# Gradient of the shift taps on VectorE over rows turned by DMA, and dh slab by slab ahead of dw, in a fused long-convolution and gated-MLP backward kernel

## The chip, the cores and the metric

One core of a Trainium2 chip runs the whole kernel. The metric is the device time of one execution in microseconds (us). Engines are written as in the profile: PE is TensorE, PEld its weight loads, DVE is VectorE, ACT is ScalarE, POOL is GpSimd, SP is SyncE, which only issues DMAs here.

## What is computed

The forward function takes x = q of shape 2048 x 1024 (rows s, channels d), normalises its rows, and forms two branches whose product is added to x. The reference returns that output and the gradients of nine of its inputs.

```python
def _A_ref(q, k, v, shift_k, ssm_k, ssm_D):
    for t in range(ks):                       # ks = 4: the shift taps
        k_shift = k_shift + k_pad[:, t:t + S, :] * shift_k[:, ks - 1 - t][None, None, :]
    kv = k_shift * v
    ...                                       # y: long causal convolution of kv with ssm_k, by FFT
    y = y + kv * ssm_D[None, None, :]
    return q * y
def _B_ref(x, w_gate, w_up, w_down):
    g = jnp.einsum("bsd,df->bsf", x, w_gate)
    u = jnp.einsum("bsd,df->bsf", x, w_up)
    return jnp.einsum("bsf,fd->bsd", g * u, w_down)
xn = _layernorm(x, axis=-1)
s = _A_ref(xn, A_k, A_v, A_shift_k, A_ssm_k, A_ssm_D)
g = _silu(_B_ref(xn, B_w_gate, B_w_up, B_w_down))
return x + s * g
...
_out, _vjp = jax.vjp(_f, A_q, A_k, A_v, A_shift_k, A_ssm_k, A_ssm_D, B_w_gate, B_w_up, B_w_down)
```

F is 3584. The gradient of the shift taps is, for each channel d and tap j, the sum over s of dkshift[s, d] * k[s - j, d].

## The kernel before, in words

A tile framework schedules the program: the author writes operations in an order, and a scheduler puts each engine's queue in an order of its own, by priorities and its own reckoning of times, unless an operation is marked to keep its place (`keep_in_program_order`, which PIN and PINQ switch on) or to follow another (`issue_after`). Each engine then works through its queue strictly in order, and so does each queue of DMA issues. Pools hand out buffers; a tile with one buffer is written again only when its last reader is done.

The work runs in five stages, in the time of the profiled execution:

1. *g and u* (0 to 580 us): PE multiplies the normalised rows by w_up and w_gate in 14 slabs of 256 columns (L585). The forward convolution is pumped in between (`conv_forward`, L608).
2. *bm* (580 to 775 us): h times w_down (L988), then `gate` (L993), which makes the output and the gradients dbm, dy, dxa.
3. *dh and dw* (775 to 1397 us): for each of 14 slabs, `dh_half` (L1108) computes two halves of dh = dbm times w_down transposed: per half, four PSUM tiles of 16 matmuls (L1119), copied by ACT (L1121), and two multiplications on DVE that turn the stored g and u into their gradients in place (L1126). `dw_slab` (L1132) then makes the weight gradients of the slab, eight groups of 16 matmuls (L1136), whose operands are both halves of the slab. The two are interleaved: after each dw group, half of a `dh_half` of the next slab is issued (`halves`, L1181), and its multiplication is issued behind the PSUM group after it (`todo`, `after_group`).
4. *dwd* (1397 to 1638 us): the gradient of w_down (L1244), 14 slabs of four groups. Each slab's h (1 MB) is loaded by SP (`load_h`, L1151), the results (wbs, four buffers) are stored by ACT's queue (L1249). Between the loads of h, SP issues DMA transposes of weights (`load_wgu`, L1199, 1 MB each) and of the stored gradients (`load_dgut`, L1204, two of 256 KB each) for the last stage. Transposes of weights wait for the latest issue of an h load.
5. *dx* (1638 to 2056 us): the gradient of the normalised rows (`dx_part`, L1264, matmuls L1267), 16 blocks of 128 rows in pairs; PSUM tile psx has three buffers. Each block ends with `ln_backward` (L1273): DVE adds psx and dxna into dxn (L1289), which frees psx, and the rest of the layer norm follows. While the second pair of every four blocks runs, SP reloads the 14 dgut pieces (28 transposes) for the next four.

The backward convolution (`conv_backward`, L838) is pumped into stages 3 and 4 by `btick`: 8 forward transforms of dy (`fwd8`, matmuls psF L230, whose PSUM is copied by ACT ahead, `fwd8_half` L268), then 16 units of product, inverse transform and matmuls (psY, L420 and L927). Its DVE work, the multiplications of stage 3 and the stores on POOL's queue are all marked to keep program order. The tail of an h unit (`dh_tail`, L918) copies PSUM by ACT in plain order into hr, and POOL turns it into ho (L931).

The gradients of k and of the shift taps come from `dk_units` (L936), pumped into stage 5: 16 units (8 groups of 128 channels, two halves of the rows). Each loads kh and dkh by POOL's queue, makes dk by seven operations on DVE (dka, dkp), and computes the taps on PE: 16 matmuls of dkh against four shifted views of kh (L964), accumulated in psdk over both halves. The taps are the diagonal of the result: DVE multiplies by `diag`, sums, and copies (L971 to L974).

Of the kernel before, what the change touches and what calls it, by code (L numbers as in the profile page):

```python
# [19 lines left out]
def build_kernel(  # L20
# [11 lines left out]
    nc = tc.nc  # L32
# [30 lines left out]
    PINQ = [False]  # L63

    def st(out, in_):
        ins = nc.gpsimd.dma_start(out=out, in_=in_)  # L66
        if PINQ[0]:
            tc.keep_in_program_order(ins)
        return ins
# [47 lines left out]
    ident_f = const.tile([P, P], F32, name="ident_f")  # L117
    make_identity(nc, ident_f[:])
# [9 lines left out]
    diag = const.tile([P, 64], F32, name="diag")  # L128
# [74 lines left out]
    PIN = [False]  # L203

    def tt(o, a, b, op):
        ins = V.tensor_tensor(o, a, b, op)  # L206
        if PIN[0]:
            tc.keep_in_program_order(ins)
# [53 lines left out]
    def stt(o, a, f, b):  # L262

        ins = V.scalar_tensor_tensor(o, a, f, b, op0=MUL, op1=ADD)
        if PIN[0]:
            tc.keep_in_program_order(ins)

    def fwd8_half(x, i, wp, psp):  # L268

        SP = wp.tile([P, 2, 2, 512], F32, name="SP", bufs=2)  # L270
        for j in range(2):
            r = 2 * i + j
            ps = psp.tile([P, 2, 2, 256], F32, name="psF")
            cmm(ps[:, 0], T4[0], x, (r,))
            cmm(ps[:, 1], T4[0], x, (r + 4,))
            nc.scalar.copy(out=SP[:, :, j], in_=ps[:].rearrange("p s k x -> p s (k x)"))
        return SP

    def fwd8(SPs, X, wp, ahead):

        W = wp.tile([P, 16, 256], F32, name="W16")
        C = wp.tile([P, 4, 256], F32, name="W4")
        for i in range(2):
            s, q = [SPs[i][:, j].rearrange("p a (k x) -> p (a k) x", k=2) for j in range(2)]
            tt(W[:, 4 * i:4 * i + 4, :], s, q, ADD)
            tt(W[:, 4 * i + 8:4 * i + 12, :], s, q, SUB)
            yield 2.5
        tt(C[:], W[:, 0:4, :], W[:, 4:8, :], ADD)
        tt(W[:, 0:4, :], W[:, 0:4, :], W[:, 4:8, :], SUB)
        ahead(0)  # L290
        yield 2.4
        dft4(C[:], W[:, 0:4, :], X, 0)
        ahead(1)
        yield 2.8

        d0, d2r = W[:, 8:10, :], W[:, 13:11:-1, :]
        tt(C[:, 0:2, :], d0, d2r, ADD)
        tt(d0, d0, d2r, SUB)
        re, im = W[:, 10:15:4, :], W[:, 11:16:4, :]
        tt(C[:, 2:4, :], re, im, ADD)  # L300
        tt(W[:, 12:14, :], im, re, SUB)
        yield 2.8
        q, pr_ = C[:, 2:4, :], W[:, 13:11:-1, :]
        tt(W[:, 10:12, :], q, pr_, ADD)
        tt(W[:, 14:16, :], q, pr_, SUB)
        stt(pr(X, 2, 15), W[:, 10:15:4, :], C8, C[:, 0:2, :])
        stt(pr(X, 10, 7), W[:, 10:15:4, :], -C8, C[:, 0:2, :])
        yield 2.9
        stt(pr(X, 6, 11), W[:, 11:16:4, :], C8, d0)
        stt(pr(X, 14, 3), W[:, 11:16:4, :], -C8, d0)  # L310
        yield 1.5
    FWD8_W = 2 * 2.5 + 2.4 + 2.8 + 2.8 + 2.9 + 1.5
# [428 lines left out]
    tt(diag[:], ident_f[:, 0:64], ident_f[:, 64:128], ADD)  # L741
# [74 lines left out]
    def dy_forward(cx, cs):  # L816
        def load(ds):
            if ds < 8:
                x = cx.tile([P, NB, P], BF16, name="dyx")
                cld(x[:], DYd[ds])  # L820
                xs_.append(x)
        xs_, sp = [], []

        def half(ds, i):
            if ds < 8:
                sp.append(fwd8_half(xs_[ds], i, cs, ps_c3))
        load(0)
        load(1)
        half(0, 0)
        half(0, 1)  # L830
        for ds in range(8):
            SPs = sp[2 * ds:2 * ds + 2]
            load(ds + 2)
            X = cs.tile([P, 16, 256], BF16, name="DX")
            yield from fwd8(SPs, X, cs, lambda i: half(ds + 1, i))
            st(DYFd[ds], X[:])

    def conv_backward():  # L838
# [54 lines left out]
        for n in range(16):  # L893
            yield from staggered(main(n), tl, 7.0)
            tl = tail(n)
# [6 lines left out]
    def dkv_tail(ds, G, tiles, ew):  # L902
        v, ksh = tiles
        y = ew.tile([P, NB, P], BF16, name="yl")
        for rp in range(4):
            ps = inv8_rows(G, ps_y4[0], rp)
            nc.scalar.copy(out=by_res(y[:], rp), in_=rowps(ps))
        yield 0.0
        yield 0.0
        tt(v[:], v[:], y[:], MUL)  # L910
        tt(ksh[:], ksh[:], y[:], MUL)
        for c in range(2):
            cs_ = slice(8 * c, 8 * c + 8)
            st(DKSHd[ds, 1024 * c:1024 * c + 1024, :].rearrange("(u r) d -> u r d", r=8), v[:, cs_, :])
            st(o_dv[:, c, :, ds * P:(ds + 1) * P], ksh[:, cs_, :])
        yield 2.5

    def dh_tail(ds, G, ew):  # L918
        hr = ew.tile([P, 2, 8, P], BF16, name="yl")
        ho = ew.tile([P, 2, P, 8], BF16, name="ho")  # L920
        for c in range(2):
            for rq in range(2):
# [6 lines left out]
                nc.scalar.activation(hr[:, c, 4 * rq:4 * rq + 4], ps[:], ACT.Copy, scale=WSC)  # L929
        yield 0.0  # L930
        nc.gpsimd.tensor_copy(ho[:], hr[:].rearrange("p c r u -> p c u r"))  # L931
        nc.gpsimd.tensor_copy(ddo[:, ds:ds + 1], hr[:, 0, 0, 0:1])
        st(o_dssmk[ds * P:(ds + 1) * P, :], ho[:].rearrange("p c u r -> p (c u r)"))
        yield 0.0

    def dk_units(ew, psp):  # L936
        def load(i):
            ds, c = divmod(i, 2)
            kh = ew.tile([P, 11, P], BF16, name="kh")
            cld_k(kh[:], c, ds)  # L940
            dk = ew.tile([P, 11, P], BF16, name="dkh")
            src = DKSHd[ds]
            cld(dk[:], bass.AP(src.tensor, src.offset + 1024 * c * P, [[8 * P, P], [P, 11], [1, P]]))
            return kh, dk

        kh, dk = load(0)
        yield 2
        for i in range(16):
# [11 lines left out]
            if c == 0:  # L960
                ps = psp.tile([P, 4, 64], F32, name="psdk")
            for r in range(8):
                for j in (slice(0, 64), slice(64, 128)):
                    nc.tensor.matmul(ps[j], dk[:, r, j], kh[:, r:r + 4, j],  # L964
                                     start=(c == 0 and r == 0), stop=(c == 1 and r == 7))
            yield 1
            if i < 15:
                kh, dk = load(i + 1)
            if c == 1:
                dt_ = ew.tile([P, 4, 64], F32, name="dt2")  # L970
                tt(dt_[:], ps[:], diag[:].unsqueeze(1).to_broadcast([P, 4, 64]), MUL)  # L971
                dr_ = ew.tile([P, 4], F32, name="dr2")
                V.tensor_reduce(dr_[:], dt_[:], AX.X, ADD)
                V.tensor_copy(dsko[:, ds, ::-1], dr_[:])  # L974
            yield 2
        st(o_dshk.rearrange("(c p) j -> p c j", p=P), dsko[:])
    DK_TOTAL = 2 + 16 * 6

    C_TOTAL = 8 * FWD8_W + 16 * (PROD_W + INV8_W) + 8 * 1.4 + 8 * 2.5
# [120 lines left out]
    todo = []  # L1100

    def after_group(n):
        flush(2)
        while todo:
            todo.pop(0)()
        btick(n)

    def dh_half(k, wdt):  # L1108
# [3 lines left out]
        for g in range(2):  # L1112
            dht = bg.tile([P, 4, SLW], BF16, name="dht", bufs=3)
            for e in range(2):
# [7 lines left out]
                after_group(1)  # L1122

            def multiply(g=g, dht=dht):
                bs = slice(4 * g, 4 * g + 4)
                tt(dgu[:, :, bs], dgu[:, :, bs], dht[:].unsqueeze(1).to_broadcast([P, 2, 4, SLW]), MUL)  # L1126
                if g == 1:
                    ld(DGd[sl, :, 1024 * hf:1024 * hf + 1024, :].rearrange("a (u b) f -> u a b f", u=P), dgu)
            todo.append(multiply)
            yield  # L1130

    def dw_slab(sl, dgus, others):  # L1132
        for dc in range(DC):
# [12 lines left out]
            after_group(2)  # L1146
            next(others, None)

    h_ld = [None]

    def load_h(sl):  # L1151
        h = u8(HSL[sl % 3], "p (b f) -> p b f", b=NB)
        h_ld[0] = ld(h, Hd[sl])
        hs[sl] = h
# [8 lines left out]
    for k in (3, 4):  # L1163
        gu_in(k)
    DBM = [u8(q, a=4) for q in (10, 8, 4, 5)]
    HSL = (3, 11, 6)
    hs = {}
    PIN[0] = PINQ[0] = True
    for k in range(2):
        run(dh_half(k, wdt))  # L1170
    todo.pop()()
    for sl in range(NSL):
        if sl + 2 < NSL:
            wdts.append(load_wdt(sl + 2))
        if sl + 1 == NSL:
# [4 lines left out]

        def halves():  # L1181
            for k in (2 * sl + 2, 2 * sl + 3):
                if k < 2 * NSL:
                    yield from dh_half(k, wdts[sl + 1])
        dw_slab(sl, [DGU[2 * sl], DGU[2 * sl + 1]], halves())
# [28 lines left out]
    for k in range(NSL):  # L1214
        if k + 2 < NSL:
            load_h(k + 2)
        with tc.issue_after(h_ld[0].ins):
# [4 lines left out]
        if k == 11:  # L1222

            bdrain()
            PIN[0] = PINQ[0] = False
# [13 lines left out]
        for f in range(2):  # L1239
# [9 lines left out]
            sta(o_dwd[f0:f0 + P, :], wbs)  # L1249
# [10 lines left out]
    ps_k = pool("ps_k", 1, space=PSUM)  # L1260
    kpump, kdrain = make_pump(dk_units(kw_, ps_k), DK_TOTAL)
# [68 lines left out]
    for p_ in (ps_k, ps_x, kw_, gs, gl, gd2, ub, ua, gd, gw):  # L1330
# [64 lines left out]
```

## Time and profile before

| What | Value |
|---|---|
| median of three runs | 2061.24 us (2058.28 to 2066.14) |
| profiled execution | 2058.28 us; its span 2056.5 us |
| busy, share of the span | PE 1969.5 us (96%), DVE 1434.8 (70%), ACT 647.8 (32%), POOL 343.7 (17%) |
| mean granted TensorE clock | 0.982 |
| chain that ended last, by line | psx L1267 18%, psb L1136 18%, psb L1119 8%, psb L1244 5%, SPq L1202 4%, psdk L964 1% |
| DMA | 440.74 MB, mean 214 GB/s |
| idle of PE ahead of L1244, released by the load of h | 20.2 us |
| idle of DVE ahead of dka, released by the load of dkh | 199.5 us, 15 times |

How to read it: busy times are sums over the span, so the stage has to be looked at before an engine is called the bound. A wait is the idle time of an engine just before an instruction, with what released it. The chain is followed back from the last instruction. "SPq" is time in which SP's queue was issuing a DMA.

### The profile page before, as it was taken

The numbers are of one execution on the slowest core, as the hardware profiler recorded it, in microseconds if no ns is written. First come the engines' busy times: TensorE is split into PE (matmuls) and PEld (weight loads), VectorE is DVE, ScalarE is ACT, GpSimd is POOL, SyncE is SP. The second block draws the span as 40 slices with busy tenths as digits, with TensorE's granted clock in tenths as the row PEclk, the third lists the DMA queues.
The fourth block names the chain that finished last, engine by engine and source line by source line (L and its number), as shares of the span: only waits on it lengthen the run. The fifth ranks groups of instructions, "written<-read, shape, count | busy, mean of one in ns | idle before, by whom it ended". The sixth has DMA issues, their size and how long they took to land.

```text
span 2056.5 us, 27740 instructions
## 1 busy us (share of the span) xinstructions
PE 1969.5 (96%) x11288; PEld 1054.7 (51%) x11288; DVE 1434.8 (70%) x1576; ACT 647.8 (32%) x954; POOL 343.7 (17%) x496
## 2 busy tenths in 40 slices
PE   6999999999999999999999999999879799999998
PEld 3455555545544446666566655654434344444443
DVE  6779898978836556886999899999953034434343
ACT  4655554546432234432222222221112101111112
POOL 3322222111112211001021212121102001010100
PEclk9999999999999999999999999999989899999999
DMA  9686666557699987655686997667997979393951
GB/s 294 217 285 218 214 212 215 197 183 244 231 289 293 290 284 259 222 196 212 237 268 225 253 253 228 241 212 206 142 242 149 205 182 209 118 195 93 189 114 57
DMA packets 422528, 440.74 MB, mean 214 GB/s; under 512 B 248960, under 2 KB 336824, under 8 KB 408576
## 3 DMA queue, kind: packets, MB, share of 16 engines
q1 hardware_dynamic: 329472, 211.06, 40.6%
q0 software_dynamic: 42112, 176.51, 26.7%
q10 hardware_dynamic: 50816, 51.39, 7.9%
q8 instruction: 88, 1.44, 0.3%
q14 instruction: 40, 0.33, 0.1%
HBM read 198.72 MB, written 189.83 MB: 189 GB/s over the span
## 4 chain that ended last, share of the span: by engine, by line
PE 60%; issue 17%; DVE 9%; SPq 5%; POOL 4%; DMA 4%; ACT 1%; ACTq 0%; POOLq 0%; DVEq 0%
PE psx L1267 18%; PE psb L1136 18%; PE psb L1119 8%; PE psg L585 5%; PE psb L1244 5%; SPq L1202 4%; DVE W L206 2%; DVE HX L206 2%; PE psF L230 2%; SPq L1209 1%; DVE m L206 1%; DVE KX L206 1%; PE psdk L964 1%; PE psY L420 1%; POOL HTd L66 1%
## 5 line engine op out<-in xcount | busy, mean ns | idle before, releaser
L585 PE MATMUL psg<-wslab,U 128*128 128x512 bf16 x1792 | 417.1, 385 | 8.4 <-ACT U L558 5.5
L1136 PE MATMUL psb<-U,U 128*128 128x512 bf16 x1792 | 396.9, 379 | 0.0
L1267 PE MATMUL psx<-U,dgut 128*128 128x512 bf16 x1536 | 337.2, 380 | 5.1 <-DVE dxn L206 3.4
L1267 PEld LDWEIGHTS <-dgut 128*128 128x128 bf16 x1792 | 174.5, 98 | 217.0 <-issue 10.7
L585 PEld LDWEIGHTS <-U 128*128 128x128 bf16 x1792 | 175.0, 99 | 201.8 <-issue 15.0
L1136 PEld LDWEIGHTS <-U 128*128 128x128 bf16 x1792 | 175.3, 98 | 199.0 <-issue 0.4
L1244 PE MATMUL psb<-U,U 128*128 128x512 bf16 x896 | 201.3, 387 | 28.8 <-DMA U<-Hd 20.2
L1119 PE MATMUL psb<-wdt,U 128*128 128x256 bf16 x1792 | 206.4, 273 | 1.1 <-ACT bm L1006 1.1
L587 ACT CAST gut<-psg 128x512 bf16<-128x512 f32 x224 | 131.4, 587 | 204.2 <-PE psg L585 189.8
L1119 PEld LDWEIGHTS <-U 128*128 128x128 bf16 x1792 | 175.6, 98 | 31.5 <-issue 1.4
L988 PE MATMUL psbm<-U,ht 128*128 128x512 bf16 x784 | 169.9, 379 | 0.0
L1141 ACT CAST wb<-psb 128x512 bf16<-128x512 f32 x112 | 65.6, 586 | 311.6 <-PE psb L1136 308.7
L1244 PEld LDWEIGHTS <-U 128*128 128x128 bf16 x896 | 88.9, 100 | 138.8 <-DMA U<-Hd 20.7
L206 DVE TENSOR_TENSOR W<-W 128x1024 f32<-128x1024 f32 (+1 forms) x144 | 149.8, 1059 | 3.0
L206 DVE TENSOR_TENSOR dka<-dkh,Wbc 128x1024 bf16<-128x1024 bf16 x16 | 11.1, 692 | 199.5 <-DMA dkh<-DKSHd 199.5
L206 DVE TENSOR_TENSOR W<-SP 128x1024 f32<-128x1024 f32 x96 | 112.4, 1221 | 43.5 <-ACT SP L245 33.6
L1290 ACT ACTIVATE dx_t<-dxn 128x1024 bf16<-128x1024 f32 (+1 forms) x17 | 17.1, 1007 | 342.8 <-DVE dxn L206 284.6
L988 PEld LDWEIGHTS <-ht 128*128 128x128 bf16 x784 | 76.6, 98 | 91.8
L1121 ACT CAST dht<-psb 128x512 bf16<-128x512 f32 x112 | 65.6, 586 | 118.2 <-PE psb L1119 106.5
L206 DVE TENSOR_TENSOR U<-U,dht 128x2048 bf16<-128x2048 bf16 x56 | 71.1, 1272 | 44.3 <-ACT dht L1121 44.3
L206 DVE TENSOR_TENSOR m<-A,B 128x2048 bf16<-128x2048 bf16 (+1 forms) x48 | 73.4, 1577 | 40.1 <-issue 23.5
L1246 ACT CAST wbs<-psb 128x512 bf16<-128x512 f32 x56 | 32.3, 587 | 197.4 <-PE psb L1244 147.2
(203 smaller groups left out, 2284.7 us busy)
## 6 DMA issues: line engine op xcount, KB each, us to landing
U<-GUd SPq DMA_DIRECT2D x28, 1024.0 KB, 8.2
DGd<-U SPq DMA_DIRECT2D x28, 1024.0 KB, 4.5
GUd<-gut ACTq DMA_DIRECT2D x54, 512.0 KB, 4.3
A<-DYFd POOLq DMA_DIRECT2D x16, 1024.0 KB, 8.9
out_dram<-wb ACTq DMA_DIRECT2D x112, 128.0 KB, 5.0
U<-Hd SPq DMA_DIRECT2D x14, 1024.0 KB, 6.7
Hd<-hN POOLq DMA_DIRECT2D x54, 256.0 KB, 4.1
HTd<-hT POOLq DMA_DIRECT2D x54, 256.0 KB, 4.0
```

Source lines behind the costliest of these rows:

```text
L206: ins = V.tensor_tensor(o, a, b, op)
L230: nc.tensor.matmul(ps[:, k].rearrange("p (c d) -> p c d", c=2), T[:, r, k, :], xr[:, r], start=(n == 0), stop=(n == len(rs) - 1 and (first ...
L585: gu_mm[0] = nc.tensor.matmul(ps[:], XNT[q][:, dc, qi * P:(qi + 1) * P], w[:, dc].rearrange("p a f -> p (a f)"), start=(dc == 0), stop=(dc ...
L587: nc.scalar.copy(out=gut[:, :, i], in_=ps[:].rearrange("p (a f) -> p a f", a=2))
L988: nc.tensor.matmul(ps[:, dh * 512:(dh + 1) * 512], ht(fc)[:, i * P:(i + 1) * P], WD[fc // 4][:, fc % 4, dh * 512:(dh + 1) * 512], start=(f ...
L1119: nc.tensor.matmul(ps[:, x * SLW:(x + 1) * SLW], DBMT[2 * hf + g][:, dc, (b % 4) * P:(b % 4 + 1) * P], wdt[:, dc, :], start=(dc == 0), sto ...
L1121: nc.scalar.copy(out=dht[:, 2 * e:2 * e + 2].rearrange("p b f -> p (b f)"), in_=ps[:])
L1136: nc.tensor.matmul(ps[:], XN[b // 4][:, b % 4, dc * P:(dc + 1) * P], dgus[b // 8][:, :, b % 8], start=(b == 0), stop=(b == NB - 1))
L1141: nc.scalar.copy(out=wb[:, dc % 2].rearrange("p a f -> p (a f)"), in_=ps[:])
L1202: nc.sync.dma_start_transpose(out=store, in_=(B_w_gate, B_w_up)[a][:, j * 512:(j + 1) * 512])
L1244: nc.tensor.matmul(ps[:], h[:, b, f * P:(f + 1) * P], DBM[b // 4][:, b % 4, dh * 512:(dh + 1) * 512], start=(b == 0), stop=(b == NB - 1))
L1267: nc.tensor.matmul(ps[:, dh * 512:(dh + 1) * 512], t[n][:, f, i * P:(i + 1) * P], WGU[n][:, f, dh * 512:(dh + 1) * 512], start=(n == 0 and ...
```

## The change

It has four parts.

*Taps.* `dk_units` no longer loads kh and no longer uses PE. For each unit SP loads k and the gradient dkshift once more by DMA transpose, as kT and dkT with channels on partitions and 1024 rows along the free axis (one buffer each). DVE computes each tap by one `scalar_tensor_tensor` with an accumulated sum over up to 1024 elements: four a unit, 64 in all, plus an addition of both halves. `diag`, `ident_f` and the pool ps_k go. The weights of the pump's steps change with it.

*dh.* `dh_half` is no longer a generator: a whole half is issued, its two multiplications at a raised priority, and `dw_slab` runs in one piece. The order is: second half of this slab, first half of the next, then dw of this slab.

*Order.* PIN and PINQ are gone: the scheduler orders DVE's and POOL's work. `fwd8` makes its own matmuls and PSUM copies instead of having them ahead. The lag of `staggered` goes from 7.0 to 6.0. `dh_tail` has ACT write ho with steps of eight elements, instead of POOL turning it.

*dwd.* Loads of h move from SP to ACT's queue, stores of wbs from ACT to SP's queue, and a transpose of weights waits for the issue of the latest store of wbs.

```diff
-        ins = nc.gpsimd.dma_start(out=out, in_=in_)
-        if PINQ[0]:
-            tc.keep_in_program_order(ins)
-        return ins
+        return nc.gpsimd.dma_start(out=out, in_=in_)
...
-    def fwd8(SPs, X, wp, ahead):
+    def fwd8(x, X, wp, psp):
...
         for i in range(2):
-            s, q = [SPs[i][:, j].rearrange("p a (k x) -> p (a k) x", k=2) for j in range(2)]
+            SP = wp.tile([P, 2, 2, 512], F32, name="SP", bufs=2)
+            for j in range(2):
+                r = 2 * i + j
+                ps = psp.tile([P, 2, 2, 256], F32, name="psF")
+                cmm(ps[:, 0], T4[0], x, (r,))
+                cmm(ps[:, 1], T4[0], x, (r + 4,))
+                nc.scalar.copy(out=SP[:, :, j], in_=ps[:].rearrange("p s k x -> p s (k x)"))
+                yield 0.1
+            s, q = [SP[:, j].rearrange("p a (k x) -> p (a k) x", k=2) for j in range(2)]
...
-                nc.scalar.activation(hr[:, c, 4 * rq:4 * rq + 4], ps[:], ACT.Copy, scale=WSC)
-        yield 0.0
-        nc.gpsimd.tensor_copy(ho[:], hr[:].rearrange("p c r u -> p c u r"))
-        nc.gpsimd.tensor_copy(ddo[:, ds:ds + 1], hr[:, 0, 0, 0:1])
+                nc.scalar.activation(ho[:, c, :, 4 * rq:4 * rq + 4].rearrange("p u r -> p r u"), ps[:], ACT.Copy, scale=WSC)
+        yield 0.4
+        nc.scalar.copy(out=ddo[:, ds:ds + 1], in_=ho[:, 0, 0, 0:1])
...
-            kh = ew.tile([P, 11, P], BF16, name="kh")
-            cld_k(kh[:], c, ds)
             dk = ew.tile([P, 11, P], BF16, name="dkh")
...
-            return kh, dk
+            kT = ew.tile([P, 1, 16 + H], BF16, name="kT")
+            t0 = 0 if c else 16
+            nc.sync.dma_start_transpose(out=kT[:, :, t0:], in_=kin[c * H - 16 + t0:c * H + H, ds * P:(ds + 1) * P])
+            dkT = ew.tile([P, 1, H], BF16, name="dkT")
+            nc.sync.dma_start_transpose(out=dkT[:], in_=DKSHd[ds, c * H:c * H + H, :])
+            return dk, kT, dkT
...
             if c == 0:
-                ps = psp.tile([P, 4, 64], F32, name="psdk")
-            for r in range(8):
-                for j in (slice(0, 64), slice(64, 128)):
-                    nc.tensor.matmul(ps[j], dk[:, r, j], kh[:, r:r + 4, j],
-                                     start=(c == 0 and r == 0), stop=(c == 1 and r == 7))
+                taps = ew.tile([P, 2, 4], F32, name="taps", bufs=2)
+            for m in range(4):
+                lo = 0 if c else 3 - m
+                prod = ew.tile([P, 8, P], BF16, name="dkp")
+                V.scalar_tensor_tensor(prod[:].rearrange("p r d -> p (r d)")[:, lo:H], dkT[:, 0, lo:H], 1.0,
+                                       kT[:, 0, 13 + m + lo:13 + m + H], op0=MUL, op1=MUL,
+                                       accum_out=taps[:, c, 3 - m:4 - m])
+                yield 1
+            if i < 15:
+                dk, kT, dkT = load(i + 1)
+            if c == 1:
+                tt(dsko[:, ds, :], taps[:, 0, :], taps[:, 1, :], ADD)
...
-                after_group(1)
-
-            def multiply(g=g, dht=dht):
-                bs = slice(4 * g, 4 * g + 4)
+                flush(2)
+                btick(1)
+            with tc.high_priority(60):
                 tt(dgu[:, :, bs], dgu[:, :, bs], dht[:].unsqueeze(1).to_broadcast([P, 2, 4, SLW]), MUL)
...
         h = u8(HSL[sl % 3], "p (b f) -> p b f", b=NB)
-        h_ld[0] = ld(h, Hd[sl])
+        sta(h, Hd[sl])
...
     for sl in range(NSL):
+        dgus = [first, dh_half(2 * sl + 1, wdts[sl])]
         if sl + 2 < NSL:
             wdts.append(load_wdt(sl + 2))
-        if sl + 1 == NSL:
+        if sl + 1 < NSL:
+            first = dh_half(2 * sl + 2, wdts[sl + 1])
+        else:
...
-        dw_slab(sl, [DGU[2 * sl], DGU[2 * sl + 1]], halves())
+        dw_slab(sl, dgus)
...
-        with tc.issue_after(h_ld[0].ins):
+        with tc.issue_after(wst.ins) if k > 0 else nullcontext():
...
-            sta(o_dwd[f0:f0 + P, :], wbs)
+            wst = ld(o_dwd[f0:f0 + P, :], wbs)
...
-    ps_k = pool("ps_k", 1, space=PSUM)
-    kpump, kdrain = make_pump(dk_units(kw_, ps_k), DK_TOTAL)
+    kpump, kdrain = make_pump(dk_units(kw_), DK_TOTAL)
```

## The prediction

> **What bounds the kernel now.** I read the table of stretches first, then the groups, then the timelines of SP and PE. The columns of the table: stretch, its length, busy us of PE, PEld, DVE, ACT and POOL, granted TensorE clock, DMA share, GB/s.
>
> ```profile
> 782.00:1397.00 615.00, 609.29 (x3848) 373.54 (x3846) 541.39 (x530) 179.80 (x294) 90.38 (x123) 0.99 0.72 230
> 1397.00:1638.00 241.00, 210.53 (x1070) 98.73 (x1069) 138.88 (x124) 42.85 (x77) 33.10 (x25) 0.93 0.95 186
> 1638.00:2056.50 418.50, 405.58 (x2038) 186.57 (x2037) 159.53 (x214) 57.50 (x85) 38.41 (x61) 0.99 0.69 146
> ```
>
> PE fills the first stretch (the dh and dw slabs) and the last (dx). The middle one (dwd) loses some 30 us, and there the DMA share is highest. So work that leaves PE in dx comes off the end, and a new PE wait anywhere adds to it. The groups of dx that the change touches or that price it:
>
> ```profile
> L964 PE MATMUL psdk<-kh,dkh 128*64 128x256 bf16 x256 | 17.2, 276 | 0.0
> ...
> L206 DVE TENSOR_TENSOR dkp<-dkh,Wbc 128x1024 bf16<-128x1024 bf16 x48 | 33.1, 689 | 0.9
> ...
> L1300 DVE SCALAR_TENSOR_TENSOR dx_t<-dxn,RSTN,dout_t 128x1024 bf16<-128x1024 f32 x15 | 19.3, 1284 | 0.4
> ```
>
> SP's timeline (start, us, then the operation) shows who stands behind whom on SP; the first three lines lie in dwd, the rest in dx:
>
> ```profile
> 1454.53 41.15 SPq L1202 DMA_TRANSPOSE U<-in_B_w_gate_dram  x1
> 1495.77 0.53 SPq L61 DMA_DIRECT2D U<-Hd  x1
> ...
> 1586.52 38.00 SPq L1209 DMA_TRANSPOSE dgut<-DGd  x12
> ...
> 1664.34 4.58 SPq L1202 DMA_TRANSPOSE U<-in_B_w_up_dram  x1
> 1669.15 0.39 SPq L61 DMA_DIRECT2D dxna_t<-DXNAd  x1
> ...
> 1706.84 34.46 SPq L1209 DMA_TRANSPOSE dgut<-DGd  x20
> ```
>
> A load of h stood 41 us behind a weight transpose: that is PE's largest hole (20.2 us before L1244, by the waits). Twenty dgut transposes of 256 KB held SP for 34.46 us, 1.72 each; alone one takes 1.22 to 1.30 to issue, and lands 4.7 us after issue in the median (3.4 to 23.6). Last, from PE's timeline, the one wait of PE in dx:
>
> ```profile
> 1845.99 12.02 PE L1267 MATMUL psx<-U,dgut 128*128 128x512 bf16 x48 [3.43 <-DVE dxn L206]
> ```
>
> Here dxn, the operation of VectorE that frees psx, stood behind a product that waited for the dkh load (8.37 us of DMA dkh in the chain just before). This is the mechanism that I expect to grow.
>
> **Part 1: psdk leaves PE.** In PE's timeline a group of 16 psdk matmuls starts at 1678.29 and the next psx at 1679.29: 1.00 us. 16 groups make **-16.0**, all on the path. The sums over the diagonal go as well, 8 x (0.42 + 0.42 + 0.17) = 8 us of DVE, worth nothing: DVE is busy 159.5 of 418.5 us there.
>
> **Part 2: 64 products with sums on DVE.** Nearest rows: 0.69 (a bf16 product of this size) and 1.28 (L1300, the same instruction with an f32 operand). I take 1.22, close to the same instruction: 4.9 us a unit, 78 in all. As throughput this hides in DVE's 259 idle us; it counts only inside the chain of part 4.
>
> **Part 3: 32 more transposes on SP.** kT and dkT hold 256 KB each like one dgut load, so I price them like it. 32 x 1.72 = 55 us of DMA in a stretch with a share of 0.69: room on the whole, none inside the dgut bursts (share 1.06 to 1.16 per 20 us).
>
> **Part 4: the wait added.** kT and dkT have one buffer. kT of unit i+1 waits on SP for the last sum of unit i, and what is queued behind it on SP (dgut, dxna, xn, dout) waits too; the sums of unit i+1 wait on DVE for both transposes, and dxn behind them, and PE for dxn. A unit's loop is two issues 2.6 + landing 4.7 + sums 4.9 = **12.2 us**; lower bound 2.4 + 3.4 + 2.8 = 8.6; with a landing of 23.6 it is 31. Before, PE itself held dk back, since psdk stood between psx groups (a unit every 1700.11 - 1678.29 = 21.8 us). That brake is gone, and in the order that the scheduler gives DVE, dk runs ahead. The first dxn stands behind units 0 to 4 and 6 of the 7 operations of unit 5's dka (before: behind units 0 and 1 and 5 operations of unit 2); the third dxn behind unit 8 and a sum of unit 9; the fifth behind unit 13.
> - First: unit 2's kT follows the last weight transposes and the first dxna, xn and dout. Those were out 32 us into dx (1670.3 against 1637.9), now with one transpose fewer ahead: 27. Three loops are 36.6, five operations of 0.69 and dxn 1.2 follow: 68.3. A pair of blocks is 224 matmuls of 0.2165 = 48.5 us of PE, and the third psx buffer gives 1.7: a hole of **18**.
> - Third: count from the first dxn's start. PE wants the third by 49.7. dout waits for dx_t, 7.3 us behind dxn before (1687.24 to 1694.52), with four sums between them now 13, and kT of unit 6 stands behind it. Three loops, then issue and landing of unit 9, 7.3; four dgut transposes stand between the halves of units 8 and 9, 6; a sum and dxn 2.4: 65.3, a hole of 15.6 in calm queues. The dgut burst runs just then, so I take **20**.
> - Fifth: no burst. 9 us of dgut and xn ahead of unit 10, four loops 48.8, dxn 1.2: 59 against 49.7, a hole of **9**.
> Together **+47**. With loops of 8.6 they are 7 + 3 + 0 = 10; with one landing of 23.6 in each of the first two, 85. After unit 15 nothing is left to wait for. The wait of 3.4 at 1845 is of this kind and is counted out: **-3.4**.
>
> **Part 5: weight transposes later.** kT of unit 1 waits on SP for the sums of unit 0, and five weight transposes stand behind it. Issued every 4.9 us (24.5 for five) and landing after 8.5 (median of the line) they come 8 to 28 us into dx; PE wants pieces 9 to 13 at 9 x 3.46 = 31 to 45. Some 17 us of cover: 0 to +20, I take **+5**.
>
> **Part 6: dh no longer interleaved.** I summed DVE's rows in its order between one slab's multiplies and the next, scaled by 0.945 (first multiply to end of convolution the sums make 735, the trace 676 busy and 20 of gaps). Before: 40 to 43 us a slab. After, from the fifth group on: 45, 49, 48, 44, 46, 44, 44, together 319, where PE needs 7 x 43.35 = 303 (1049.09 to 1092.44 in the chain). Following both sums, with DVE waiting for dh where it is early, DVE comes 7 us after PE's need at the eighth slab and 9.5 at the last; before it had 15 in hand. **+10**. Bounds: 0, and +35 (DVE stood idle 1 to 10% from 1000 to 1400, some 23 us in all; no slack takes that up now).
>
> **Part 7: dwd.** h loads move to ACT's queue, wbs stores to SP behind the weight transposes. The hole at 1482 to 1504, 22 us, loses its cause. A wbs store behind 41 us leaves PE 4 wbs of 6.9 and 4 psb of 3.45 = 41 of cover, less 18 (the stores' median landing in that stretch): some comes back. At the end, stores 22 to 24 stand behind 2 weight and 15 dgut transposes; a like row of them took 51 us (1573.64 to 1624.5), and PE loses some 15 there already. **-10**; bounds -24 and +25. The activation that writes ho in steps costs between 0.60 (L929) and 0.97 (a quarter of POOL's 3.89), x32; ACT is busy 18 to 30%, which hides it, and if not, 12 us. POOL loses 31 us that nobody on the path waited for.
>
> **Sum** against the profiled execution (2058.28; span 2056.5): -16.0 + 47 - 3.4 + 5 + 10 - 10 = +32.6, 2090.9. The median of the runs shown is 3.0 above that execution: **2094**.
>
> **A rule against the change.** The dgut row turns 8 blocks of 128x128 in 1.72 us. The Trainium skill, "VectorE: DVE Perf Modes", The three transpose paths, puts one block at 1309 ns by DMA and 390 by TensorE. By it a transpose would be 10.5 us, a loop 26, and the end near 2,240. For dgut's shape this trace disagrees; for rows of 256 bytes it shows nothing.
>
> **Rivals.**
> - *Faster.* The chain is short: unit 2's transposes out by 20 us (not 27) and loops of 8.6 leave the first dxn at 50.5, as PE wants it, and nothing after it late. Then 16, 3.4 and dwd's 22 come off: 2061.3 - 41.4 = **2020**. For: DMA is at 0.2 to 0.5 between bursts. Against: six weight transposes took SP 30 us after dx began. 0.13.
> - *No change*: loops of 8.6, all else as forecast: -16 - 3.4 + 10 + 5 + 10 - 10 = -4.4, **2057**. 0.14.
> - *Much slower*: two landings of 23.6 and part 6 at its bound: -16 - 3.4 + 85 + 5 + 35 - 10 = +95.6, **2157**. For: DVE is busy 97 and 96% from 1300 to 1500. 0.18.
> - The forecast, 2072 to 2130: 0.55.
> Chances with a bound of 0.5%, about what a measurement of this kernel can tell from no change: faster 0.13, within 0.14, slower 0.73. The range 2048 to 2150 leaves out most of the first and half of the third.
>
> **What would show it.** Waits of PE L1267 on DVE dxn in the first three pairs, falling; landings of kT and dkT near 5 us; no hole at L1244 that names U<-Hd; DVE nearly without idle from 1000 to 1400, and PE short of 100% by some 10 us there. Sums of 0.69, or units out on SP without gaps, break part 4; PE idle of over 35 us from 1000 to 1400 breaks part 6.

## The result, and the profile after

The changed kernel takes 2122.56 us (median of four runs, 2108.10 to 2126.82), 1.0284 of the kernel before (95% interval 1.0231 to 1.0337; its four runs beside it had a median of 2060.75). The forecast was 2094, slower, with a range to 2150. All ratios in this document are taken over the executions within 1.5% of the fastest of the same kernel. The profiled execution took 2123.78, its span 2121.8.

The table of stretches of the changed kernel, with the same three stages in its own times (columns as before: stretch, length, busy us of PE, PEld, DVE, ACT and POOL, granted TensorE clock, DMA share, GB/s):

```profile
782.00:1423.00 641.00, 617.64 (x3854) 375.84 (x3852) 544.39 (x543) 200.76 (x298) 75.74 (x118) 0.98 0.68 223
1423.00:1658.00 235.00, 207.36 (x1058) 97.64 (x1057) 113.49 (x112) 77.55 (x82) 8.20 (x14) 0.94 0.95 177
1658.00:2121.80 463.80, 395.53 (x1792) 177.09 (x1791) 227.72 (x325) 57.74 (x86) 29.80 (x45) 0.93 0.66 142
```

In dx PE runs fewer matmuls (x1792 for x2038), as meant, yet the stretch has grown from 418.5 to 463.8 and the clock has fallen from 0.99 to 0.93. dh and dw have grown too, dwd is shorter. From first matmul to first matmul of the next stage: dh and dw 625.6 to 650.7 (+25.1), dwd 240.5 to 235.1 (-5.4), dx 418.6 to 463.5 (+44.9); with 0.7 lost ahead of them this is the whole 65.3 between the spans.

The waits of PE in these stages (operation and line, what it waited for, us in total, times, longest):

```profile
PE psx L1222 <- DVE dxn L196: 51.7, 3, 27.9
PE psb L1099 <- DVE U L196: 16.1, 7, 4.1
PE psx L1222 <- ACT wbs L1202: 11.1, 1, 11.1
PE psb L1200 <- ACT wbs L1202: 10.1, 1, 10.1
PE psx L1222 <- DMA U<-in_B_w_up_dram: 6.8, 1, 6.8
PE psb L1200 <- DMA U<-Hd: 6.6, 1, 6.6
```

The single wait of 3.43 for dxn has become three that hold 51.7. PE's timeline has them falling from pair to pair, 27.90, 20.25, 3.51 us, and none after:

```profile
1698.17 21.51 PE L1222 MATMUL psx<-U,dgut 128*128 128x512 bf16 x88 [6.82 <-DMA U<-in_B_w_up_dram]
1747.58 17.25 PE L1222 MATMUL psx<-U,dgut 128*128 128x512 bf16 x72 [27.90 <-DVE dxn L196]
...
1817.89 17.93 PE L1222 MATMUL psx<-U,dgut 128*128 128x512 bf16 x72 [20.25 <-DVE dxn L196]
...
1872.13 15.70 PE L1222 MATMUL psx<-U,dgut 128*128 128x512 bf16 x72 [3.51 <-DVE dxn L196]
```

psdk is gone from the groups. What stands in its place, and one row that nobody had asked for:

```profile
L939 DVE SCALAR_TENSOR_TENSOR dkp<-dkT,kT 128x1024 bf16<-128x1024 bf16 (+2 forms) x64 | 78.3, 1223 | 64.4 <-DMA dkT<-DKSHd 63.1
L899 ACT ACTIVATE yl<-psY 128x512 bf16<-128x512 f32 x32 | 74.7, 2712 | 0.0
```

A sum takes 1.22 us, as taken, and DVE sat idle 63 us ahead of the sums for dkT. The second row is the write of ho in steps of eight elements: 2.71 us against 0.60 for the contiguous write before.

SP's timeline of the changed kernel at the start of dx (dx begins at 1658.3):

```profile
1666.61 1.30 SPq L915 DMA_TRANSPOSE kT<-in_A_k_dram  x1
1667.95 2.44 SPq L917 DMA_TRANSPOSE dkT<-DKSHd  x1
1670.49 4.32 SPq L1159 DMA_TRANSPOSE U<-in_B_w_gate_dram  x1
1674.91 0.53 SPq L61 DMA_DIRECT2D out_dram<-wbs  x1
1678.19 1.18 SPq L915 DMA_TRANSPOSE kT<-in_A_k_dram  x1
...
1711.83 1.19 SPq L915 DMA_TRANSPOSE kT<-in_A_k_dram  x1
1713.05 2.23 SPq L917 DMA_TRANSPOSE dkT<-DKSHd  x1
1722.46 1.16 SPq L915 DMA_TRANSPOSE kT<-in_A_k_dram  x1
...
1732.34 1.16 SPq L915 DMA_TRANSPOSE kT<-in_A_k_dram  x1
```

The second unit's kT waits from 1675 to 1678 for the first unit's sums, with five weight transposes and two stores of wbs behind it. Then, from 1711.83, units come every 10.6 and 9.9 us while dxn waits behind them on DVE. The first dxn starts at 1746.31, 88 us into dx, behind the sums of five units and six of the seven operations that make the sixth's dka, as the prediction had read the order; in the kernel before it started 49 us into dx.

### The profile page after: what moved, and what is told of

Same layout as the page of the kernel before. It is cut to its first block, busy times and chain, and to the rows that moved or that the text cites. A ratio compares the mean times of both kernels' runs of the same rounds, so it can differ in the third digit from the quotient of the medians.

```text
span 2121.8 us, 27360 instructions
## 1 busy us (share of the span) xinstructions
PE 1962.8 (93%) x11032; PEld 1045.7 (49%) x11032; DVE 1480.0 (70%) x1687; ACT 703.0 (33%) x962; POOL 294.3 (14%) x462
## 5 line engine op out<-in xcount | busy, mean ns | idle before, releaser
L1099 PE MATMUL psb<-U,U 128*128 128x512 bf16 x1792 | 399.1, 383 | 16.1 <-DVE U L196 16.1
L1222 PE MATMUL psx<-U,dgut 128*128 128x512 bf16 x1536 | 341.9, 385 | 69.6 <-DVE dxn L196 51.7
L1099 PEld LDWEIGHTS <-U 128*128 128x128 bf16 x1792 | 176.7, 99 | 226.4 <-issue 25.8
L1084 PE MATMUL psb<-wdt,U 128*128 128x256 bf16 x1792 | 199.8, 273 | 1.1 <-ACT bm L978 1.1
L196 DVE TENSOR_TENSOR W<-W 128x1024 f32<-128x1024 f32 (+1 forms) x144 | 139.2, 986 | 2.8
L939 DVE SCALAR_TENSOR_TENSOR dkp<-dkT,kT 128x1024 bf16<-128x1024 bf16 (+2 forms) x64 | 78.3, 1223 | 64.4 <-DMA dkT<-DKSHd 63.1
L196 DVE TENSOR_TENSOR dxn<-psx,dxna_t 128x1024 f32<-128x1024 f32 (+1 forms) x17 | 19.7, 1160 | 126.5 <-PE psx L1222 122.7
L1086 ACT CAST dht<-psb 128x512 bf16<-128x512 f32 x112 | 65.3, 586 | 128.9 <-PE psb L1084 105.7
```

What stands on the lines that cost most here:

```text
L939: V.scalar_tensor_tensor(prod[:].rearrange("p r d -> p (r d)")[:, lo:H], dkT[:, 0, lo:H], 1.0, kT[:, 0, 13 + m + lo:13 + m + H], op0=MUL, ...
L1084: nc.tensor.matmul(ps[:, x * SLW:(x + 1) * SLW], DBMT[2 * hf + g][:, dc, (b % 4) * P:(b % 4 + 1) * P], wdt[:, dc, :], start=(dc == 0), sto ...
L1086: nc.scalar.copy(out=dht[:, 2 * e:2 * e + 2].rearrange("p b f -> p (b f)"), in_=ps[:])
L1099: nc.tensor.matmul(ps[:], XN[b // 4][:, b % 4, dc * P:(dc + 1) * P], dgus[b // 8][:, :, b % 8], start=(b == 0), stop=(b == NB - 1))
L1222: nc.tensor.matmul(ps[:, dh * 512:(dh + 1) * 512], t[n][:, f, i * P:(i + 1) * P], WGU[n][:, f, dh * 512:(dh + 1) * 512], start=(n == 0 and ...
```

## The experiments

Theory A is the prediction's: dxn stands on DVE behind sums that wait for transposes, and that costs more than psdk gave back; part 6 adds some. The rivals put the loss on the queues that were swapped in dwd (B), on the 32 transposes themselves (C), and on issue and landing of the transposes in place of the length of the sums, which is part of A's loop (D). For dh and dw, part 6's lost interleaving stands against the scheduler's order alone (E), both together (F), and both together with fwd8 no longer ahead (G).

| Kernel | ratio to before (95%) | dh and dw | dwd | dx | PE waits for dxn |
|---|---|---|---|---|---|
| before | 1 | 625.6 | 240.5 | 418.6 | 3.4 |
| after | 1.0284 (1.0231 to 1.0337) | 650.7 | 235.1 | 463.5 | 51.7 |
| e1 before, new taps | 1.0216 (1.0144 to 1.0288) | 625.7 | 220.9 | 458.4 | 51.7 |
| e2 after, old taps | 1.0132 (1.0075 to 1.0189) | 644.7 | 230.2 | 416.0 | none |
| e3 before, dwd queues swapped | 1.0123 (1.0037 to 1.0209) | 624.4 | 257.6 | 415.5 | none |
| e4 after, dwd queues as before | 1.0362 (1.0276 to 1.0448) | 645.5 | 231.3 | 451.7 | 47.1 |
| e5 e1 with DVE order held | 0.9955 (0.9918 to 0.9992) | 625.6 | 224.6 | 409.2 | 6.8 |
| e6 e1 with short sums | 1.0202 (1.0120 to 1.0285) | 625.5 | 240.0 | 449.5 | 46.1 |
| e7 before, dh grouped | 0.9996 (0.9961 to 1.0031) | 624.3 | 218.7 | 414.5 | 0.8 |
| e8 before, order not held | 0.9980 (0.9943 to 1.0018) | 626.8 | 229.9 | 415.0 | 1.4 |
| e9 both of these | 0.9996 (0.9954 to 1.0038) | 638.9 | 221.4 | 418.9 | 3.6 |
| e10 e9 with the new fwd8 and lag | 1.0081 (1.0046 to 1.0116) | 652.1 | 226.4 | 413.8 | 0.2 |
| e11 after with DVE order held | 1.0090 (1.0044 to 1.0137) | 649.5 | 231.1 | 409.0 | 3.1 |
| e12 before, ho written in steps | 0.9969 (0.9931 to 1.0006) | 631.7 | 221.6 | 423.8 | 5.3 |

Stages are us of one profiled execution each. The dwd column has to be read with care: e1, e5, e6 and e7 leave dwd as it was, and it took 220.9, 224.6, 240.0 and 218.7 us. The medians of before beside these kernels were 2044.71 (e1 to e4), 2044.40 (e5 to e8) and 2048.05 (e9 to e12), with single runs from 2027.75 to 2074.87. So ratios, not times, are compared across the three groups.

### The taps

**e1, the new taps alone.** The edit puts after's `dk_units` into the kernel before, and takes `diag`, `ident_f` and ps_k out.

> The kernel before with the taps alone changed (sums on VectorE over kT and dkT, no psdk); dh interleaved, the pins and the dwd queues stay. Theory A (the chain kT, dkT, sums, dxn on SP and DVE costs more than psdk gave back): in the profile of after dx is 45 us longer than before, so about 2105 us (2095 to 2118), with PE waits for dxn of 40 to 55 us in all and none at psb of the dh and dw stage. Rival B (dx is late because wbs stores and h loads changed queues, so that the transposes on SP start late): 2045 to 2075, PE waits for dxn below 15 us.

Measured: dx 458.4, 40 us longer than before's 418.6, with the same 51.7 us of waits for dxn as in after (26.3, 23.0, 2.4), though the queues of dwd are untouched:

```profile
PE psx L1265 <- DVE dxn L203: 51.7, 3, 26.3
```

Theory A stands for dx and B falls. The median, 2078.39, lies under the 2095 to 2118 expected, but before's beside it was lower too (2044.71, where the expectation had built on 2060.75); the ratio, 1.0216, is what the expected 45 us make.

**e2, everything but the taps.** The old `dk_units` in the changed kernel.

> The kernel after with the taps of before (kh loaded, psdk on PE); all else as after. Theory A: after less 45, about 2078 us (2068 to 2090), PE waits for dxn below 6 us, waits at psb on DVE in the dh and dw stage as in after (some 16 us). Rival B: still 2100 to 2125.

Measured: dx 416.0 and no wait for dxn; PE's waits at the dw matmuls for DVE 12.5. A as expected, but for the median, 2066.44, just under the 2068 to 2090; before's beside it was lower too. What stays of the loss, 1.0132, belongs to the other parts.

**e5, the same taps with VectorE's order held.** dk's operations, the sums and dxn are marked to keep program order:

```diff
-                V.scalar_tensor_tensor(prod[...], dkT[...], 1.0, kT[...], op0=MUL, op1=MUL, accum_out=...)
+                tc.keep_in_program_order(
+                    V.scalar_tensor_tensor(prod[...], dkT[...], 1.0, kT[...], op0=MUL, op1=MUL, accum_out=...))
...
-            tt(dxn[:, cl], ps, dxna_t[:, cl], ADD)
+            tc.keep_in_program_order(V.tensor_tensor(dxn[:, cl], ps, dxna_t[:, cl], ADD))
```

(and likewise the operations that make dka, and the addition of both halves)

> The kernel before with the new taps, and on VectorE dk's operations, the sums and dxn kept in program order, so that about two units stand ahead of the first dxn instead of almost six. Theory A, order on VectorE (dxn stands behind sums that wait for transposes): PE waits for dxn fall from 51.7 us to below 10, dx from 458 us to 405 to 415, so some 45 us under the kernel with the new taps alone and 0 to 15 us under before. Rival C (the transposes themselves, 32 more through SP and the DMA engines, make dgut, dxna, xn and the sums late whatever the order): waits of PE in dx of 30 us or more, dx 435 us or more, within 15 us of the kernel with the new taps alone.

Measured: the same 32 transposes, the same 64 sums. PE's waits from 1600 on are these two, the first of them just ahead of dx, which begins at 1621.8; the third line is DVE's first dxn:

```profile
PE psx L1267 <- ACT wbs L1247: 7.4, 1, 7.4
PE psx L1267 <- DVE dxn L1289: 6.8, 4, 4.1
...
1671.22 1.22 DVE L1289 TENSOR_TENSOR dxn<-psx,dxna_t 128x1024 f32<-128x1024 f32 x1 [25.73 <-PE psx L1267]
```

dx is 409.2, 49 us under e1, and the whole kernel 0.9955 of before (0.9918 to 0.9992). That is no shown gain over before: over all executions its median is 2044.89 and before's 2044.40. DVE's first dxn starts at 1671.22, 49 us into dx, behind the sums of two units, where it waits for nothing but PE, instead of 78 us into it behind five units in e1. C falls: the transposes cost little in themselves. This is the experiment that shows the mechanism, since it changes nothing but the order on one engine.

**e11, the changed kernel with the same order held.**

> The kernel after with, on VectorE, dk's operations, the sums and dxn kept in program order. Theory A: PE waits for dxn fall from 51.7 us to below 10 and dx from 463.5 us to 405 to 420; the stage of dh and dw stays at 645 to 651; some 45 us under after, 10 to 25 us over before. Rival C (swapped queues and 32 more transposes make it late anyway): waits for dxn above 25 us, dx 435 us or more.

Measured: dx 409.0, waits for dxn 3.1, ratio 1.0090. In the changed kernel, too, the order on VectorE alone is worth what theory A says: 463.5 to 409.0 in dx. The 0.9% that stays goes with dh and dw, still at 649.5.

**e6, sums over 128 elements.**

```diff
-                V.scalar_tensor_tensor(prod[:].rearrange("p r d -> p (r d)")[:, lo:H], dkT[:, 0, lo:H], 1.0,
-                                       kT[:, 0, 13 + m + lo:13 + m + H], op0=MUL, op1=MUL,
+                V.scalar_tensor_tensor(prod[:].rearrange("p r d -> p (r d)")[:, lo:128], dkT[:, 0, lo:128], 1.0,
+                                       kT[:, 0, 13 + m + lo:13 + m + 128], op0=MUL, op1=MUL,
```

> The kernel before with the new taps, each sum over 128 elements instead of 1024: seven eighths of each sum are left out, the transposes stay whole. Part 4's loop of a unit was issue 2.6 + landing 4.7 + sums 4.9 = 12.2 us; with sums of some 0.25 us it is 8.3, and the prediction's lower bound (loops of 8.6) gave holes of 10 us in all in place of 47. So theory A: PE waits for dxn of 5 to 20 us, dx 415 to 430, 25 to 45 us under the kernel with the new taps alone. Rival D (issue and landing behind other transposes set the loop, and sums lie beside them): waits for dxn stay above 35 us.

Measured: waits for dxn 46.1, ratio 1.0202, as e1. Neither theory had the reason right. SP's timeline of this kernel has the loop about as short as A worked out (8.3 us):

```profile
1696.71 1.20 SPq L942 DMA_TRANSPOSE kT<-in_A_k_dram  x1
...
1704.97 1.24 SPq L942 DMA_TRANSPOSE kT<-in_A_k_dram  x1
...
1713.57 1.30 SPq L942 DMA_TRANSPOSE kT<-in_A_k_dram  x1
```

(The differences are 8.26 and 8.60, and 6.76 and 6.15 just ahead of them; in e1 they are 10.11, 9.73 and 9.97.) But the scheduler's order has changed too: the sums of seven units stand ahead of the first dxn in place of five, and it starts 78.5 us into dx, against 77.9 in e1. So shorter work was filled up with more work; that the scheduler reckons the shorter sums cheaper is the likely reason, not a tested one. The prediction's lower bound for the holes (10 us with loops of 8.6) left the order as it was, and that is not what a shorter operation gets.

### The queues of dwd

**e3, the swap alone.**

```diff
-        h_ld[0] = ld(h, Hd[sl])
+        sta(h, Hd[sl])
...
-        with tc.issue_after(h_ld[0].ins):
+        with tc.issue_after(wst.ins) if k > 0 else nullcontext():
...
-            sta(o_dwd[f0:f0 + P, :], wbs)
+            wst = ld(o_dwd[f0:f0 + P, :], wbs)
```

> The kernel before with the queues of dwd alone changed (h loaded by ACT's queue, wbs stored by SP, weight transposes after the latest store). Part 7 of the prediction: -10 (-24 to +25); the stages of after measured -5 (dwd with the gap to dx 235 against 240), so 2051 to 2058, the 20 us hole that names U<-Hd gone and in its place a wait for wbs of 10 to 20 us. Rival: the stores behind the transposes cost more than the hole did, 2065 to 2085.

Measured: 1.0123 (1.0037 to 1.0209), on the rival's side, but not clear: its four executions run from 2048.55 to 2076.22, before's seven beside them from 2027.75 to 2074.87. SP's timeline and PE's waits in dwd:

```profile
1452.57 62.40 SPq L1202 DMA_TRANSPOSE U<-in_B_w_gate_dram  x1
1515.06 1.46 SPq L61 DMA_DIRECT2D out_dram<-wbs  x2
```

```profile
PE psb L1244 <- ACT wbs L1246: 39.3, 2, 32.3
```

One weight transpose held SP for 62.40 us, two stores of wbs stood behind it, and PE waited 32.3. Before, the load of h stood behind the like of it (41.15 us, hole 20.2). The swap changes who stands behind the transpose, not that someone does. In e1, with before's queues, the transpose at the same place took 10.07 us and there was no such hole. So the long transpose is an event of some executions, and PE's 32.3 us with it. What sets its length was not found.

**e4, the changed kernel with the old queues.**

> The kernel after with the queues of dwd as before. Part 7: after plus 5 to 10, 2127 to 2133 us. Rival (the swap holds up SP at the start of dx, so that the first unit's transposes come late): 2095 to 2115, with the first hole on dxn, 27.9 us in after, at 18 or below.

Measured: 1.0362 (1.0276 to 1.0448), dwd 231.3, first hole on dxn 22.6. The interval overlaps after's. The median, 2108.96, is in the rival's range, but before's beside it was lower too, and the hole is above the rival's 18. In the changed kernel the swap neither gains nor loses anything that these runs can tell, and it does not cause the holes of dx.

**e12, ho in steps.** In the kernel before, ScalarE writes ho as in after; POOL's turn goes.

> The kernel before with ho written by ScalarE in steps of eight elements, without POOL's turn. In after this write took 2.71 us (0.60 contiguous), four a unit, 87 us in all in place of 19. Part 7 hid it: the stages within 5 us of before's (625.8, 219 to 240, 415 to 419) and no PE wait that names yl above 3 us. Rival: psY and psb copies stand behind it on ScalarE, and PE loses the 12 us that the prediction gave for that case, or more.

Measured: 2.74 us a write, 75 us busy in all in place of 17 (writes that overlap are counted once), and 0.9969 (0.9931 to 1.0006). No wait of PE names yl. The work is hidden. The 6 us more in dh and dw of this execution are not explained by it as far as the waits go: 4.4 of them are a longer wait for the load of dyx at its beginning.

### dh and dw

**e7, dh grouped, order still held.** `dh_half` and `dw_slab` of after in the kernel before.

> The kernel before with dh alone changed as in after (a whole half at a time ahead of dw, its DGd store behind both multiplications), VectorE and the GpSimd queue still held in program order. Theory A of part 6 (grouping takes the slack that interleaving gave the multiplications): the stage of dh and dw is 10 to 25 us longer than before's 625.8, with PE waits at the dw matmuls on VectorE. Rival E (the loss of the 25 us in after is the scheduler's order on VectorE): within 4 us of before.

**e8, order not held, dh still interleaved.** The edit is one line:

```diff
-    PIN[0] = PINQ[0] = True
```

> The kernel before without the holding of VectorE and the GpSimd queue in program order; dh stays interleaved, fwd8 stays ahead. Theory A of part 6: the stage of dh and dw within 4 us of before's 625.8. Rival E (the scheduler's order on VectorE makes the multiplications late): 10 to 25 us longer, with PE waits at the dw matmuls on VectorE.

**e9, both, and e10, both with after's fwd8, dy loads and lag.**

> The kernel before with dh grouped as in after and without the holding in program order, both at once; each alone left the stage of dh and dw at 624 to 627 us. Theory F (the two together: the scheduler puts convolution work ahead of grouped multiplications): the stage at 640 to 651 us, with 10 us or more of PE waits at the dw matmuls on VectorE. Rival G (fwd8's own matmuls and copies, no longer ahead, are needed for the loss): within 5 us of 625.8.

> As the kernel just before this one, with fwd8 and the convolution's lag of after as well: all of after's changes to the stage of dh and dw but the strided write of ho; taps and dwd queues as before. Theories F and G both: the stage at 643 to 651 us, waits at the dw matmuls on VectorE of 12 to 17 us, dx within 4 us of 415, so 15 to 25 us over before. If the stage stays within 5 us of 625.8, the strided write of ho, which alone is missing, made the loss.

Measured: e7 624.3 us and 0.9996, e8 626.8 and 0.9980: neither alone costs anything that can be told, so part 6's theory (grouping alone) and E (order alone) both fall as put. e9 is 0.9996 (0.9954 to 1.0038); its profiled execution took 2067.00 against its median of 2043.91, and its 638.9 is that of a long execution. By the times F falls and G holds: the pair costs nothing that can be told. e10 has the whole loss of this stage: 652.1 us, 1.0081 (1.0046 to 1.0116), and these waits:

```profile
PE psb L1113 <- DVE U L206: 18.0, 8, 6.1
...
PE psY L415 <- DVE B L264: 5.6, 2, 5.4
```

So beside the other two it takes fwd8's change and the lag to make the loss; whether these make it alone, no run shows. DVE now comes late with the multiplications. One place where it stands idle shows on POOL's queue, which issues the convolution's loads, here of its tiles A and B. The kernel before (start, us, operation, idle before and its releaser):

```profile
1131.48 0.74 POOL L66 DMA_DIRECT2D B<-HFd  x1
...
1142.70 0.55 POOL L66 DMA_DIRECT2D A<-DYFd  x1 [5.08 <-DVE W L206]
```

with this on its DVE:

```profile
1126.73 1.22 DVE L206 TENSOR_TENSOR vl<-vl,yl 128x2048 bf16<-128x2048 bf16 x1
```

The changed kernel:

```profile
1135.38 0.55 POOL L64 DMA_DIRECT2D A<-DYFd  x1 [21.19 <-DVE W L196]
1137.78 0.55 POOL L64 DMA_DIRECT2D DKSHd<-vl  x1 [1.85 <-DVE vl L196]
...
1141.02 0.74 POOL L64 DMA_DIRECT2D B<-HFd  x1
```

and on its DVE:

```profile
1136.26 1.22 DVE L196 TENSOR_TENSOR vl<-vl,yl 128x2048 bf16<-128x2048 bf16 x1
...
1152.02 4.57 DVE L196 TENSOR_TENSOR m<-A,B 128x4096 bf16<-128x4096 bf16 x3 [8.53 <-DMA B<-HFd]
```

Held in order, the load of B goes out 17 us ahead of its product (1148.82 on DVE). Not held, it goes out 11 us ahead, and DVE stands idle for 8.53. A load of A now stands ahead of it and waits 21 us for DVE to release its buffer, but that is not what holds this B: behind A the queue waits 1.85 us more for vl, whose stores stood ahead of B before as well. DVE made vl at 1126.73, ahead of its operations on W, and now makes it at 1136.26, behind some of them. So here it is DVE's own new order that makes its load late.

From 1100 to 1425 DVE waited 35.5 us for B in after, and none before. 16.1 of them are two cases like this one, 9.0 are two in which B stands directly behind a load of A that waited for DVE, and 10.3 are one in which B's buffer was held by PE (psY) for 9.51. The multiplications of dh stand behind, and PE behind them. But these waits do not tell the kernels with the loss from those without: DVE waited 9.6 us for B in e8, 27.9 in e9 and 23.6 in e10. So they are part of what makes DVE late, as read from the traces; which change takes up the slack that e9 still had, fwd8 without its lead or the lag, stays open.

## Why the prediction was right, and where it was not

The direction, the main mechanism and the range were right; the time was 29 us short, and the reason given for dh and dw was wrong. By steps, with what each measured:

- **Part 1, psdk -16: right, by this count.** e5's dx is 5.9 us under e8's (409.17 against 415.03), with 6.8 us of waits for dxn against 1.4. Two runs of matmuls after a wait took 2.5 and 2.6 us longer (19.94 against 17.43 for 78, 18.29 against 15.70 for some 70). 5.9 + 5.4 + 5.1 = 16.4.
- **Parts 2 and 3: right.** Sums 1.22 us. kT landed 3.6 us after issue in the median, dkT 4.2, and the median issues were 1.18 and 1.29 (1.16 to 3.07 in all); 4.7 was taken for the landing.
- **Part 4, +47: right, 51.7.** The three holes were forecast as 18, 20 and 9 and came as 27.9, 20.3 and 3.5. The first is larger because unit 2's kT was out 53.5 us into dx (1711.83 - 1658.3), not 27; the loop is shorter than 12.2 (9.9 to 10.6). e5 and e11 show that the order on VectorE is the cause. That psdk on PE had been the brake on that order is read from the traces (a unit every 21.8 us before) and not tested by itself. The lower bound was reasoned wrongly, as e6 showed.
- **Part 5, +5: 6.8 in after**, the wait for the weights at 1698 (3.4 in e11). In e1 and e4, with the stores of wbs off SP, it is none, so the wait of kT that part 5 named does not make it alone.
- **Part 6, +10: the step that failed, in size and in its reason.** It measured +25.1, inside its bounds. "Following both sums" took DVE's work as the only thing that makes the multiplications late. DVE's work from 775 us to the start of dwd is the same (548 before, 551 us after), and the sign that the prediction named, DVE nearly without idle from 1000 to 1400, did not come: it was busy 366.1 of these 400 us, 376.8 before. Grouping, the reason given, costs nothing alone (e7, 624.3), so the right sign is in part luck. The traces show DVE idle for loads of B that go out late, some of them by DVE's own new order, which the prediction did not follow; what decides the loss stays open between fwd8's lead and the lag.
- **Part 7, -10: not borne out.** The -5.4 of the profiled pair compares with an execution of before that had the hole of 20 us. With the same queues e1, e5, e8 and e12 had no such hole, e7 one of 0.7 and e6 one of 13.0; in after, where none was to name the load of h, one of 6.6 does. The swap measured 1.0123 alone (e3, not clear) and 1.0362 when undone in the changed kernel (e4, where after has 1.0284): no gain is shown. The write of ho took 2.71 us where 0.60 to 0.97 was allowed; that it is hidden was right (e12).
- **Not in the sum:** after most waits the matmuls run slower at first, by some 1.5 to 2.8 us each time (below). In dx, -16 + 51.7 - 3.4 + 6.8 make 39.1 of the 44.9, and these slower runs are of the size of the rest.

So dx came to +44.9 (forecast +32.6), dh and dw to +25.1 (+10), dwd to -5.4 (-10): the misses all lie on one side.

## What to carry to other kernels

Taking work off the bounding engine can also take away the brake that paced other work: when the moved work no longer needs PE, look at what the scheduler now puts ahead of the operation that frees PE's buffers, and hold that order by hand before judging the move. When a queue's order is let go, follow each queue that it held, the ones that only issue loads too. A hole seen in one execution should be seen in a second before its removal is counted as a gain.

## What the runs showed of the hardware

After most waits of over 2.4 us PE ran at half clock for some 3 to 6 us. The table of short stretches right after the wait of 27.90 in the changed kernel (columns as above; the clock stands third from the end):

```profile
1747.58:1750.58 3.00, 3.00 (x8) 1.05 (x8) 2.97 (x5) 2.30 (x4) 0.87 (x1) 0.50 0.84 250
1750.58:1753.58 3.00, 3.00 (x15) 1.36 (x14) 2.75 (x5) 1.24 (x1) 0.00 (x0) 0.97 0.60 133
```

Eight matmuls in the first 3 us, fifteen in the next. In e5, after a wait of 4.13, the clock was 0.50 and 0.54 for two such stretches; after one of 3.51 in the changed kernel 72 matmuls took the usual 15.70. A wait of only 2.42 in e1 was followed by 0.50 for 3 us (17.32 for the same run of matmuls), one of 2.19 in e11 by the usual 15.70. The Trainium skill, "TensorE: Matmul & The Clock Gate", Part 1, says that the array drops to half clock after an idle window of about 3.4 us and is back after one busy window, and that the window runs free, so that the cost varies. The varying cost agrees with these rows; the figure does not, since 2.42 us are shorter than such a window and e5's half clock lasted some 6 us.

The activation that writes 128x512 bf16 out of PSUM took 0.60 us when it wrote contiguously (before) and 2.71 and 2.74 us when it wrote every eighth element (after, e12).

A weight transpose of 1 MB held SP for 10 us in e1 and for 41 and 62 us at the same place in before and e3. What decides it stays open.
